# One remainder modulo 512 bytes for every operand that TensorE reads from SBUF

## The chip, the core and the metric

The kernel runs on one core of a Trainium2 chip. The time is that of the device, in microseconds, from one launch; several executions are timed, and their median is the figure. The kernel before takes 2820.65 us (three runs, 2819.92 to 2821.26).

## The reference

Two layers on 8 sequences of 3008 rows with 256 channels, in fp32 accuracy:

```python
X = np.fft.rfft(x, axis=1)                    # 3008 = 47 * 64
Yr = Xr @ w_r - Xi @ w_i + b_r
Yi = Xr @ w_i + Xi @ w_r + b_i
Y  = soft(Yr) + 1j * soft(Yi)                 # soft threshold at 0.01
y  = np.fft.irfft(Y, n=3008, axis=1)
t  = y.reshape(24064, 256)
out = (sigmoid(t @ w_gate) * (t @ w_val)) @ w_out     # d_ff = 1536
```

## The kernel before

The Fourier transform is a product with a 47-point table (`fa_sb`, line 176), then one with 64-point tables (`mf_sb`, line 237); between them the data goes through DRAM. The complex mixing (lines 271 and 293) follows, then the way back (`mi_sb`, lines 305 to 310, and `fb_sb`, line 340). The gated layer has its two first matrices split into a high and a low part (`w1h`, `w1l`), and the second likewise (`w2`); each product is three matmuls, high by high, high by low, low by high. Their operands are of type fp32r (one pass of TensorE); the four transforms at lines 176, 237, 305 and 340 are plain fp32, which TensorE runs as two passes, so the trace shows two matmul records for each.

The kernel runs in three stages, which the texts below name by number:

- **Stage 1**, the first 105 us: the first sequence's transform, in plain fp32, with the mixing by `mix4` (line 293).
- **Stage 2**, 105 to 1071 us: the transforms of the other seven sequences as side work (`fwd_b`, `mix`, `inv_b`, `inv_a`), put between steps of the gated layer for the first 4608 tokens (`ffn1`, lines 399 to 401, moving operands `yth` and `ytl`; `ffn2`, lines 427 to 429, moving operands `hh` and `hl`). A planner hands out the side work by fixed weights per step.
- **Stage 3**, 1071 us to the end: the gated layer for the other 19456 tokens, two blocks of 512 tokens at a time with Strassen's scheme of seven products. Its unit is a *half* (`half`, 228 of them). On TensorE a half is 33 matmuls of 512 columns: twelve in the first four products (`a11`, `s2`, `s3`, `s1`; line 659), twelve in `second` (lines 634 to 636, weights `w2`, moving `hh` and `hl`), nine in the last three products (`a12`, `s4`, `a22`; line 659 again). The four sums of a half gather in the PSUM banks `pa`, `pb`, `pc`, `pd`. Of `pd` there is one buffer only: the next half's `s3` product may start once VectorE's addition at line 720 has read it.

On VectorE, the last three additions or products of a half are lines 710, 714 and 720 in that order. On ScalarE, `put` (line 616) copies finished outputs at the end of each pair of blocks, once in twelve halves.

All memory in SBUF comes from pools. `const` and the pools `cw`, `p2`, `p4` grow from the lower end, `p0`, `p3`, `p5` (`side="right"`) from the upper end downwards. In every partition a tile is one run of bytes, and the address of a tile is the same in all partitions. The built program lists the addresses. Each matmul reads two operands from SBUF, the moving one and the stationary one (the weights). Modulo 512 bytes they start at:

| tiles | remainder before |
|---|---|
| `w1h`, `w1l`, `w2`, `th`, `tl`, `fa_sb`, `fb_sb` (weights or tables), `a11` to `a22`, `s1` to `s4`, `spare` (moving) | 128 |
| `hh`, `hl` in stages 2 and 3, `xf0`, `wi_sb` | 480 |
| `yth`, `ytl`, `vf`, `w_sb` | 0 |
| `xf`, `xfh`, `mf_sb`, `zf`, `xsh`, `xsl`, `yc`, `yh`, `yl`, `mi_sb`, `zero` | 32 |

A slice of a tile that TensorE reads begins a multiple of 512 bytes after the tile, but for the weights of `mix4` (line 293), half of which begin 256 bytes later.

Three `ffn2` steps of stage 2 are left over and run in the first halves of stage 3; their moving operand lies in `spare`, not in `hh` and `hl`:

```python
if c == NPL - 1 and f >= NF - BEHIND:
    hh, hl = (spare[f - NF + BEHIND][:, i, :CW] for i in range(2))
```

Of the kernel before, what the change touches and what calls it, by code (L numbers as in the profile page):

```python
# [9 lines left out]
F32 = mybir.dt.float32  # L10
# [9 lines left out]
R2, R1 = 47, 64  # L20
NK2 = 24
NQ = 2 * NK2
# [87 lines left out]
def tile_fft_mix_ffn(ctx: ExitStack, tc, x, w_r, w_i, b_r, b_i, w_one, w_out, mf, mi, mis, fa, fb, out):  # L110
# [3 lines left out]
    P = 128  # L114
    XR = x.shape[2]
    CT = D // P
# [4 lines left out]
    UT = 2 * PT  # L121
# [6 lines left out]

    const = ctx.enter_context(tc.tile_pool(name="const", bufs=1))

    p0s = ExitStack()
    p0 = p0s.enter_context(tc.tile_pool(name="p0", bufs=1, side="right"))
    p3s = ExitStack()
    fft = ExitStack()
    cw = fft.enter_context(tc.tile_pool(name="cw", bufs=1))
# [5 lines left out]
    def bank(name, tag="fft", bufs=FFT_BANKS):  # L141
        return (psf if tag == "fft" else psl).tile([P, 512], F32, tag=tag, bufs=bufs, name=name)
# [4 lines left out]
    def r2k(name):  # L147
        return p2.tile([P, 2, D], F32R, tag="r2k", bufs=NR2K, name=name)

    fa_sb = cw.tile([2 * R2, 2 * NQ], F32, name="fa_sb")  # L150
    nc.scalar.dma_start(fa_sb, fa)

    zd = [tc.dram_tile([NQ, R1, D], F32, name=f"zd{b}") for b in range(B)]
# [174 lines left out]
    def split_y(c, at, n, y):  # L328
        if c not in yts:
            yts[c] = [p3.tile([P, CT, CW], F32R, name=t) for t in ("yth", "ytl")]  # L330
        yh, yl = (t[:, :, at:at + n] for t in yts[c])
        nc.scalar.copy(yh, y)
        sub(yl, y, yh)

    def inv_a(u):
        vf = held.pop(("v", u))
        pa = bank("pia")[:, :CT * UT].rearrange("p (c h k) -> p c h k", c=CT, h=2)
        for hh in range(2):
            for ct in range(CT):
                nc.tensor.matmul(pa[:, ct, hh], vf[:, hh, ct * P:(ct + 1) * P], fb_sb[:, :PT], start=True, stop=True)  # L340
        py = pa.rearrange("p c h k -> p c (h k)")
        lo = u * UT
        n = 0
        if lo < T0:
            c, at = divmod(lo, CW)
            n = min(UT, CW - at)
        if 0 < n < UT and lo + n < T0:
            t = p3.tile([P, CT, UT], F32, name="carry", bufs=1)[:, :, :UT - n]
            nc.scalar.copy(t, py[:, :, n:])
            held["carry", c + 1] = t, UT - n  # L350
        if n:
            split_y(c, at, n, py[:, :, :n])
        if lo + UT > T0:
            t = result("yf")
            t = t[:, :CT * (UT - n)].rearrange("p (c k) -> p c k", c=CT)
            nc.scalar.copy(t, py[:, :, n:])
            nc.sync.dma_start(yd[:, :, lo + n - T0:lo + UT - T0], t)

    def result(name):
        return p3.tile([P, CW], F32, tag="ry", bufs=NYF, name=name)  # L360
# [123 lines left out]
    def ffn_units():  # L484
        units, todo = [], {}
        seq = [(c, f) for c in range(NPL) for f in range(NF)]

        def own(c):

            return range(-(-c * CW // UT), -(-(c + 1) * CW // UT))  # L490

        for c in range(1, NPL):
            at = (c - 1) * NF
            for i, u in enumerate(own(c)):
                todo.setdefault(at + (0, 3, 6)[i], []).append(lambda u=u: load_v(u))
                todo.setdefault(at + (3, 6, 9)[i], []).append(lambda u=u: inv_a(u))
            todo.setdefault(at + 1, []).append(lambda c=c: carry(c))

        def unit(n):
            c, f = seq[n]  # L500
            if n == 0:
                for i, u in enumerate(own(0)):
                    if i == 1:
                        w = w1h[:, 0].rearrange("p i t n -> p (i t n)")
                        keep_warm(bank("warm", "l1", L1_BANKS), w[:, :P], w, WARM_V)
                    inv_a(u)
            ffn1(c, f)
            for t in todo.pop(n, ()):
                t()
            if n >= LAG and n - LAG < len(seq) - BEHIND:  # L510
                ffn2(*seq[n - LAG])
        return [lambda n=n: unit(n) for n in range(len(seq))], own(0), own(NPL - 1)[-1] + 1
# [228 lines left out]

    bias_sb = cw.tile([P, 2, D], F32, name="bias_sb")
    bias4 = p0.tile([P, D], F32, name="bias4")
    ebias = cw.tile([P, 1], F32, name="ebias")
    fb_sb = const.tile([2 * NQ, P], F32, name="fb_sb")
    w1h = const.tile([P, NF, 2, CT, P], F32R, name="w1h")
    w1l = const.tile([P, NF, 2, CT, P], F32R, name="w1l")
# [183 lines left out]
    p3 = p3s.enter_context(tc.tile_pool(name="p3", bufs=2, side="right", reuse_waits="tile"))  # L931
# [18 lines left out]
    def inverse(g):  # L950

        us = [u for b in g for u in range(b * H // 2, (b + 1) * H // 2) if u >= u0]
        ahead = min(NVF - 1, len(us))

        def begin():
            for u in us[:ahead]:
                load_v(u)

        def go(i):
            if i + ahead < len(us):  # L960
                load_v(us[i + ahead])
            inv_a(us[i])
        return [(0.0, begin)], [(0.65, lambda i=i: go(i)) for i in range(len(us))]

    def behind(g):

        loads, units = inverse(g)
        return (loads, 0.05, 0.05), (units, 0.1, 1)

    def merge(*streams):  # L970

        return [u for _, _, u in sorted(((lo + (hi - lo) * (i + 0.5) / len(s), k, u) for k, (s, lo, hi) in
                                         enumerate(streams) for i, u in enumerate(s)), key=lambda t: t[:2])]

    (a3, q3), (a4, q4) = (fft_units(g, {}) for g in groups[3:])
    n = len(a3) // 3
    side = (merge((second_fft, 0, 1), (a3[:n], 0.2, 1)) +
            merge((third_fft, 0, 1), (a3[n:], 0, 0.85), *behind(groups[1])) +
            merge((q3, 0, 1), (a4, 0, 0.85), *behind(groups[2])) +
            merge((q4, 0, 1), *behind(groups[3])))  # L980
# [9 lines left out]
    for j in range(NF, len(ffn)):  # L990
        c, f = divmod(j, NF)
# [39 lines left out]
    a, b, c, d = banks[0]  # L1031
# [4 lines left out]
    with tc.manual_schedule():  # L1036
        for k in range(2 * NPR * NH):
            p, e = divmod(k, 2 * NH)
# [18 lines left out]
        n = NPR * NH  # L1057
# [36 lines left out]
```

## Time and profile before

| what | value |
|---|---|
| median of the runs | 2820.65 us |
| span of the profiled execution, and mean granted clock | 2819.0 us, 0.999 |
| TensorE busy | 2802.4 us (99%), 13896 matmul records |
| VectorE, ScalarE, GpSimd busy | 2082.3 (74%), 1309.6 (46%), 710.5 us (25%) |
| DMA, mean over the span | 85 GB/s |

The profile holds one execution. The only time it gives for it is the span from the first to the last instruction, 2819.0 us, which is 1.65 us under the median of the runs. A row of instructions has the line and engine, the operation, "out<-in" by tile name, the shapes, the count, then the summed busy time and the mean of one in ns, then the idle time ahead of it and what ended that. Matmuls overlap, so "mean ns of one" of a matmul (some 390 ns for 512 columns) is longer than the distance between two starts; the distance is read from the starts in the timeline. "PE" is the matmuls, "PEld" the loads of weights ahead of them.

### The profile page before, as it was taken

Reading aid. Unit: us, or ns where it says so; the run is one execution under the profiler, and the core shown is the slowest. Engines: PE = TensorE matmul, PEld = TensorE weight load, DVE = VectorE, ACT = ScalarE, POOL = GpSimd, SP = SyncE. Lnnn points to the kernel's source line nnn. Section 1 sums busy time; section 2 is a strip of 40 time slices with the busy share of each in tenths; the row PEclk is TensorE's granted clock in tenths of the full one; section 3 lists DMA queues with packets and bytes.
Section 4 is the critical chain, followed back from the end, with each engine's and each line's share of the span. In section 5 each row is a group of like instructions: output and inputs, shape, how many; then the busy total and the mean of one; then the engine's idle time right before and its main releaser. Section 6 shows DMA issues by size and latency. Waiting matters only on the chain.

```text
span 2819.0 us, 38251 instructions
## 1 busy us (share of the span) xinstructions
PE 2802.4 (99%) x13896; PEld 2308.1 (82%) x13896; DVE 2082.3 (74%) x3109; ACT 1309.6 (46%) x2276; POOL 710.5 (25%) x638
## 2 busy tenths in 40 slices
PE   9999999999999999999999999999999999999999
PEld 6678888888899888888888888888888888888887
DVE  5777778667787536777777777777777777777776
ACT  4664544545455444444444444444444444444443
POOL 0211010224100002333333333333333343333321
PEclk9999999999999999999999999999999999999999
DMA  9866544666554661000000000000000000000000
GB/s 296 257 213 194 170 143 149 199 184 192 165 152 140 186 187 38 30 15 16 30 31 27 4 31 31 31 16 15 31 30 16 15 30 31 30 1 30 30 16 15
DMA packets 173469, 241.01 MB, mean 85 GB/s; under 512 B 14592, under 2 KB 124896, under 8 KB 173280
## 3 DMA queue, kind: packets, MB, share of 16 engines
q1 hardware_dynamic: 163776, 214.93, 24.8%
q0 software_dynamic: 9408, 23.60, 2.5%
q8 instruction: 110, 1.80, 0.3%
q14 instruction: 79, 0.65, 0.1%
q10 hardware_dynamic: 96, 0.04, 0.0%
HBM read 134.17 MB, written 104.33 MB: 85 GB/s over the span
## 4 chain that ended last, share of the span: by engine, by line
PE 94%; DVE 2%; DMA 2%; ACT 1%; issue 0%; SPq 0%; DVEq 0%; ACTq 0%
PE pd L659 11%; PE pa L659 11%; PE pc L659 11%; PE po L636 8%; PE po L635 8%; PE po L634 8%; PE pm L271 6%; PE pb L659 5%; PE pia L340 4%; PE pb L237 3%; PE pa L176 2%; PE pg L399 2%; PE pg L401 2%; PE pg L400 2%; PE pv L399 2%; PE pv L400 2%
## 5 line engine op out<-in xcount | busy, mean ns | idle before, releaser
L636 PE MATMUL po<-hl,w 128*128 128x512 f32 x912 | 362.5, 397 | 0.0
L635 PE MATMUL po<-hh,w 128*128 128x512 f32 x912 | 361.5, 396 | 0.0
L634 PE MATMUL po<-hh,w 128*128 128x512 f32 x912 | 360.8, 396 | 0.0
L718 POOL TENSOR_TENSOR c<-c,c 128x512 f32<-128x512 f32 x114 | 147.7, 1296 | 831.0 <-DVE c L714 640.1
L659 PE MATMUL pa<-a,w1h 128*128 128x512 f32 x912 | 284.0, 393 | 0.0
L659 PE MATMUL pc<-s,w1h 128*128 128x512 f32 x912 | 283.7, 392 | 0.0
L714 DVE TENSOR_TENSOR c<-u,pc 128x512 f32<-128x512 f32 x228 | 156.7, 687 | 114.7 <-PE pc L659 106.2
L689 DVE TENSOR_TENSOR u<-u,pb 128x512 f32<-128x512 f32 x228 | 155.3, 681 | 88.8 <-PE pb L659 62.6
L606 ACT CAST hh<-v 128x512 fp32r<-128x512 f32 x114 | 70.7, 620 | 306.2 <-DVE v L699 306.2
L636 PEld LDWEIGHTS po<-hl,w 128*128 128x128 f32 x912 | 171.5, 188 | 41.9
L634 PEld LDWEIGHTS po<-hh,w 128*128 128x128 f32 x912 | 172.0, 189 | 40.9
L635 PEld LDWEIGHTS po<-hh,w 128*128 128x128 f32 x912 | 171.0, 188 | 40.8
L659 PEld LDWEIGHTS pa<-a,w1h 128*128 128x128 f32 x912 | 171.2, 188 | 40.1
L659 PEld LDWEIGHTS pc<-s,w1h 128*128 128x128 f32 x912 | 171.0, 188 | 37.6
L610 POOL TENSOR_TENSOR hl<-c,hh 128x512 fp32r<-128x512 f32 x114 | 152.4, 1337 | 186.1 <-ACT hh L606 186.1
L271 PE MATMUL pm<-w_sb,xsh 128*128 128x256 f32 x1008 | 189.4, 288 | 1.4 <-ACT xf L177 1.1
L659 PE MATMUL pc<-s,w1l 128*128 128x512 f32 x456 | 177.5, 389 | 0.0
L659 PE MATMUL pa<-a,w1l 128*128 128x512 f32 x456 | 177.0, 388 | 0.0
L720 DVE TENSOR_TENSOR u<-u,pd 128x512 f32<-128x512 f32 x228 | 156.9, 688 | 24.5 <-DVE c L714 0.9
L693 DVE TENSOR_TENSOR v<-v,pc 128x512 f32<-128x512 f32 x228 | 156.6, 687 | 24.4 <-DVE v L691 0.5
L691 DVE TENSOR_TENSOR v<-u,pd 128x512 f32<-128x512 f32 x228 | 156.9, 688 | 24.0 <-DVE u L689 0.5
L685 ACT COPY u<-pa 128x512 f32<-128x512 f32 x228 | 133.7, 586 | 78.7 <-PE pa L659 78.6
(174 smaller groups left out, 6738.7 us busy)
## 6 DMA issues: line engine op xcount, KB each, us to landing
zf<-zd SPq DMA_DIRECT2D x96, 256.0 KB, 3.6
vf<-vd SPq DMA_DIRECT2D x128, 192.0 KB, 3.1
out_dram<-ot SPq DMA_DIRECT2D x93, 256.0 KB, 2.2
vd<-vz SPq DMA_DIRECT2D x84, 256.0 KB, 2.9
ypair<-yd SPq DMA_DIRECT2D x19, 1024.0 KB, 5.0
yd<-yf SPq DMA_DIRECT2D x103, 188.0 KB, 3.0
xf<-in_x_dram SPq DMA_DIRECT2D x48, 384.0 KB, 4.1
zd<-xf SPq DMA_DIRECT2D x44, 384.0 KB, 3.4
```

What stands on the lines that cost most here:

```text
L271: nc.tensor.matmul(o, l, r, start=(i == 0), stop=(i == len(mms) - 1))
L610: sub_(hl, h, hh)
L634: nc.tensor.matmul(o, wh, hh, start=(f == 0), stop=False)
L635: nc.tensor.matmul(o, wl, hh, start=False, stop=False)
L636: nc.tensor.matmul(o, wh, hl, start=False, stop=(f == NF - 1))
L659: nc.tensor.matmul(o, l, r, start=not more and l is wh and r is xh, stop=l is wl, skip_group_check=more)
L689: add(u, u, b)
L691: add(v, u, d)
L693: add(v, v, c)
L714: add(c12, u, c)
L718: nc.gpsimd.tensor_mul(c12, g12, c12)
L720: add(u, u, d)
```

## The change

Four edits, all of them to where tiles lie:

```diff
+    edge = ctx.enter_context(tc.tile_pool(name="edge", bufs=1, side="right"))
+    edge.tile([P, 88], F32, name="edge")
     p0s = ExitStack()
     p0 = p0s.enter_context(tc.tile_pool(name="p0", bufs=1, side="right"))
...
-    fa_sb = cw.tile([2 * R2, 2 * NQ], F32, name="fa_sb")
+    fa_sb = cw.tile([2 * R2, P], F32, name="fa_sb")[:, :2 * NQ]
...
-            t = p3.tile([P, CT, UT], F32, name="carry", bufs=1)[:, :, :UT - n]
+            t = p3.tile([P, 3 * P], F32, name="carry", bufs=1)[:, :CT * UT].rearrange("p (c k) -> p c k", c=CT)[:, :, :UT - n]
...
-    ebias = cw.tile([P, 1], F32, name="ebias")
+    ebias = cw.tile([P, P], F32, name="ebias")[:, :1]
```

A tile `edge` that nobody uses takes 352 bytes at the upper end of each partition, so that everything in `p0`, `p3` and `p5` lies 352 bytes lower. The table `fa_sb` goes from 384 to 512 bytes, `ebias` from 4 to 512, `carry` from 1504 to 1536. In the built program every operand of TensorE then starts at remainder 128 modulo 512, but for the same half of the weights of `mix4`, which are at 384.

The instructions of each engine stand in the same order as before, with the same shapes and counts: 13214 on TensorE, 4426 on VectorE, 3199 on ScalarE, 1482 on SyncE. What each waits for is the same too, but for three waits of GpSimd on DMAs, before additions at line 586 in the first pair of stage 3, where a neighbouring tile's old transfer is now another one; one of these waits is an instruction more.

## The prediction

> **What bounds the kernel now.** First the table by stretch, cut at the stages (busy us of each engine with counts, then the granted clock, the DMA share and GB/s):
>
> ```profile
> 0.00:105.00 105.00, 97.30 (x546) 72.87 (x546) 68.07 (x116) 52.13 (x94) 12.86 (x23) 1.00 0.90 276
> 105.00:1071.00 966.00, 961.44 (x5805) 818.43 (x5804) 676.92 (x1167) 484.90 (x836) 125.52 (x189) 1.00 0.59 178
> 1071.00:2819.00 1748.00, 1743.64 (x7549) 1416.83 (x7548) 1337.35 (x1826) 772.54 (x1346) 572.08 (x426) 1.00 0.07 23
> ```
>
> TensorE has a gap of 4.4 us in all of stage 3, and VectorE, the next, works 1337 of 1748 us. The list of waits of TensorE in stage 3 has one entry, for the one buffer of `pd`:
>
> ```profile
> PE pd L659 <- DVE u L720: 0.4, 1, 0.4
> ```
>
> So stage 3 lasts as long as its matmuls stand apart: 1743.64 us by 7549 are 231.0 ns each. All have 512 columns and one pass, the clock is 1.00, and yet they aren't equal. The groups of TensorE in that window, different shapes apart:
>
> ```profile
> L636 PE MATMUL po<-hl,w 128*128 128x512 f32 x912 | 362.5, 397 | 0.0
> L635 PE MATMUL po<-hh,w 128*128 128x512 f32 x912 | 361.5, 396 | 0.0
> L634 PE MATMUL po<-hh,w 128*128 128x512 f32 x912 | 360.8, 396 | 0.0
> L659 PE MATMUL pa<-a,w1h 128*128 128x512 f32 x912 | 284.0, 393 | 0.0
> L659 PE MATMUL pb<-s,th 128*128 128x512 f32 x456 | 140.4, 389 | 0.0
> L428 PE MATMUL po<-spare,w 128*128 128x512 f32 x6 | 2.3, 389 | 0.0
> ```
>
> `pb`, with both operands at remainder 128, takes 389 ns; the `po` rows, with the moving operand at 480 and `w2` at 128, 396 to 397. Line 428 is the comparison within one line of code: from `spare` (128) 389 ns, while the same line in stage 2 reads `hh` at 480 and takes 396:
>
> ```profile
> L428 PE MATMUL po<-hh,w 128*128 128x512 f32 x210 | 83.1, 396 | 0.0
> ```
>
> The distances come from the starts in the timeline, here one half of stage 3 and a piece of the first halves:
>
> ```profile
> 2006.08 0.62 PE L659 MATMUL pa<-a,w1h 128*128 128x512 f32 x2
> ...
> 2008.80 0.40 PE L634 MATMUL po<-hh,w 128*128 128x512 f32 x1
> ...
> 2011.62 0.63 PE L659 MATMUL pa<-a,w1h 128*128 128x512 f32 x2
> ...
> 2013.69 0.62 PE L659 MATMUL pa<-a,w1h 128*128 128x512 f32 x2
> ```
>
> ```profile
> 1075.18 0.39 PE L427 MATMUL po<-spare,w 128*128 128x512 f32 x1
> ...
> 1076.54 0.62 PE L659 MATMUL pa<-a,w1h 128*128 128x512 f32 x2
> ```
>
> The first twelve matmuls of the half (all at 128) take 2008.80 − 2006.08 = 2.72 us, **226.7 ns** each. The twelve of `second` take 2.82 us, 235 each. The nine after them, again at 128, take 2.07 us, 230 each: the disturbance outlives its cause and dies out within nine matmuls. The six from `spare` take 1.36 us, 226.7 each. What two reads could meet is seen in the loads:
>
> ```profile
> 2045.31 0.41 PEld L659 LDWEIGHTS pd<-s,th 128*128 128x128 f32 x2
> ```
>
> ```profile
> 2045.31 0.39 PE L659 MATMUL pb<-s,tl 128*128 128x512 f32 x1
> 2045.53 0.62 PE L659 MATMUL pd<-s,th 128*128 128x512 f32 x2
> ```
>
> The weights for `pd` are loaded from the moment at which the matmul before begins to stream. I take it that the two reads disturb each other least when they start at the same remainder.
>
> [...]
>
> **The change part by part.** The base is the span of 2819.0 us; a run's median is 1.65 us more.
>
> *Stage 3.* A half now takes 2013.69 − 2006.08 = 7.61 us; 33 × 226.7 ns are 7.48. That is 0.13 us by 228 halves: **−29.6 us**. The whole stretch at 226.7 instead of 231.0 ns would give 7549 × 4.3 = 32.5; this also counts a few stalls that stay. Below, 0 if address has no part in it.
>
> *Stage 2, 512 columns.* `yth` goes from 0, `hh` from 480 to 128. An undisturbed run:
>
> ```profile
> 866.23 0.40 PE L399 MATMUL pg<-yth,w1h 128*128 128x512 f32 x1
> ...
> 869.72 1.05 PE L237 MATMUL pb<-mf_sb,zf 128*128 128x128 f32 x8
> ```
>
> 15 matmuls in 3.49 us, 232.7 each. Of such there are 1296 at lines 399 to 401 and 630 at 427 to 429, less those from `spare`, some 1910: 6.0 ns on each would be 11.5 us. But these runs have 6 to 18 matmuls and follow other shapes; if each has to settle like the nine above (230 ns), a run of 18 saves 18 × 6.0 − 9 × 3.3 = 78 of 108 ns, a run of six only 16 of 36. I take **−7 us**, between −3 and −11.5.
>
> *256 columns, the part against the change.* The products of line 271 (moving 0, weights 32) and those of lines 308 to 310, which have 32 and 32 already:
>
> ```profile
> 862.03 0.28 PE L271 MATMUL pm<-w_sb,xsl 128*128 128x256 f32 x1
> ...
> 863.92 0.28 PE L308 MATMUL pi<-yh,mi_sb 128*128 128x256 f32 x1
> ```
>
> ```profile
> 280.96 0.28 PE L309 MATMUL pi<-yl,mi_sb 128*128 128x256 f32 x1
> ...
> 281.56 0.59 PE L176 MATMUL pa<-xf,fa_sb 94*96 94x512 f32 x1
> ```
>
> Line 271: 16 in 1.89 us, 118.1 ns. The equal remainders: 5 in 0.60 us, 120.0. So here alignment costs some 1.9 ns, on 1512 matmuls of line 271, the 288 of line 293 (half of them) and, for settling sooner, a little on the 504 of lines 308 to 310: **+3 us**, between 0 and +3.5. A gain is not seen at any equal pair of this width.
>
> *The one buffer of `pd`.* TensorE gets faster, VectorE's chain of lines 710, 714, 720 does not. A usual half:
>
> ```profile
> 2042.57 0.39 PE L659 MATMUL pa<-a,w1l 128*128 128x512 f32 x1
> ```
>
> ```profile
> 2042.99 0.69 DVE L710 TENSOR_TENSOR g<-g,pa 128x512 f32<-128x512 f32 x1 [0.39 <-PE pa L659]
> 2043.75 0.69 DVE L714 TENSOR_TENSOR c<-u,pc 128x512 f32<-128x512 f32 x1
> 2044.55 0.69 DVE L720 TENSOR_TENSOR u<-u,pd 128x512 f32<-128x512 f32 x1
> ```
>
> The chain ends at 2045.24, and the load for `pd` starts at 2045.31, 0.07 later. From `pa` at 2042.57 to `pd` at 2045.53 TensorE has 13 matmuls in 2.96 us; at 226.7 they take 2.95. Only 0.01 to 0.02 of the 0.07 go, about what the signal needs to spare. If the load slipped in each of the some 95 odd halves and the matmuls had to settle again (0.03 us as above), it would cost 2.9: **+0.5**, between 0 and +2.9. Once in twelve halves ScalarE's output copies hold the chain up:
>
> ```profile
> 2006.75 0.58 ACT L616 COPY ot<-po 128x512 f32<-128x512 f32 x1 [0.66 <-DMA out_dram<-ot]
> ```
>
> ```profile
> 2012.72 0.68 DVE L710 TENSOR_TENSOR g<-g,pa 128x512 f32<-128x512 f32 x1
> 2014.10 0.69 DVE L720 TENSOR_TENSOR u<-u,pd 128x512 f32<-128x512 f32 x1
> ```
>
> Here line 720 ends at 2014.79, and there is no slack. From that copy the chain keeps its pace, while TensorE's matmuls up to then get some 0.13 us quicker. In these 19 halves up to 0.13 us is given back: **+1.5**, between 0 and +2.5. Next late then is `pd`'s `s3` product, with VectorE's line 720 as what ends the wait.
>
> *Nothing:* the unused 352 bytes and the padding move no data; `fa_sb` is loaded once, the same bytes; three waits of GpSimd name older transfers, and GpSimd has 572 us of work in 1748. Of the two-pass products line 237 has equal remainders (32 and 32) and 128 columns, line 340 unequal ones (128 and 0) and 94 columns, and they come out alike at 275 and 273 ns, so I count nothing there. Stage 1 waits for DMA at 0.90 share, whatever TensorE does.
>
> ```profile
> L340 PE MATMUL pia<-fb_sb,vf 96*128 96x94 f32 x1011 | 128.2, 273 | 1.2 <-DVE ys L277 0.5 <-DVE yt L273 0.5 <-ACT xsf L249 0.2
> L237 PE MATMUL pb<-mf_sb,zf 128*128 128x128 f32 x672 | 88.6, 275 | 0.0
> ```
>
> Sum: −29.6 − 7 + 3 + 0.5 + 1.5 = −31.6; 2819.0 + 1.65 − 31.6 = **2789** us. Its own bounds: all gains and no cost, −32.5 − 11.5 = −44, 2777; least of both, −29.6 − 3 + 3.5 + 2.9 + 2.5 = −23.7, 2797.
>
> **The rivals.** *(A) VectorE becomes the bound of stage 3.* If a wait at `pd` comes up in every second half, not in each twelfth, 114 × 0.13 = 15 us of the 29.6 go back: 2804. Against it: VectorE waits 0.39 us for `pa` at line 710, so its chain starts from TensorE, not from its own backlog.
>
> *(B) Not the remainder but the region.* All moving operands with 226.7 ns lie lower in SBUF than `hh`, `hl`, `yth`. If distance or the upper region is what costs, nothing is gained: 2820 to 2824. Against it: line 271's `w_sb` lies low, is unequal and doesn't settle at one distance, while lines 308 to 310 do. [...]
>
> *(C) Equal remainders collide.* In the 256-column rows the equal pair is the slower one. The longest single distance in a `second` is 240 ns:
>
> ```profile
> 2009.74 0.40 PE L635 MATMUL po<-hh,w 128*128 128x512 f32 x1
> 2009.98 0.40 PE L636 MATMUL po<-hl,w 128*128 128x512 f32 x1
> ```
>
> If all of `hh`, `hl`, `yth` and `ytl` came to stand there, it would be 5 ns × 2736 in stage 3, 7 × 1910 in stage 2, and the 3 of line 271: +30, 2851. It decides from the point at which the `po` rows stay above 396 ns. `spare` at 389 speaks against it.
>
> **How the numbers follow.** Forecast 0.75, (A) 0.11, (B) 0.10, (C) 0.04. The range 2778 to 2803 holds the forecast but for its last edge and most of (A). A difference under 0.2% (5.6 us) can't be told from none here. Faster: forecast and (A), with a little of (B): 0.87; same 0.10; slower 0.03.
>
> **What would show it.** Right: the `po` rows at 389 ns, as `spare` now; a half of 7.48 us; stage 3 near 1718 us; line 428 at 389 to 392 in stage 2; distances of 120 ns at line 271; the wait of `pd` on line 720 with some 20 entries. Wrong: `po` still at 396 (B) or above (C); `pd` waiting in over 100 halves (A); line 271 faster than 118 ns.

## The result and the profile after

| | before | after |
|---|---|---|
| median of the runs | 2820.56 us (2819.92 to 2821.26, 4 runs) | 2789.93 us (2788.98 to 2792.41, 4 runs) |
| ratio | | 0.9893, 95% interval 0.9879 to 0.9907 |
| span of the profiled execution | 2819.0 us | 2788.3 us |

The change takes 30.6 us off the median and 30.7 us off the profiled span. The forecast was 2789 us. After the change all line numbers up to 130 stay, those behind `edge` grow by two (line 634 is now 636).

The table by stretch of the kernel after, cut at the stages again (busy us of each engine with counts, granted clock, DMA share, GB/s):

```profile
0.00:105.00 105.00, 98.45 (x541) 74.30 (x541) 68.00 (x116) 52.27 (x94) 12.85 (x23) 0.98 0.89 274
105.00:1066.50 961.50, 957.07 (x5811) 820.89 (x5810) 676.19 (x1167) 485.44 (x836) 125.92 (x189) 1.00 0.60 179
1066.50:2788.30 1721.80, 1716.68 (x7549) 1414.59 (x7547) 1337.64 (x1826) 771.76 (x1346) 571.18 (x426) 1.00 0.07 23
```

Stage 3 goes from 1748.0 to 1721.8 us (−26.2), stage 2 from 966.0 to 961.5 (−4.5). Stage 1 stays but for some 0.6 us: its 546th matmul starts at 104.98 us before and at 105.54 after, in a stretch with a granted clock of 0.98 instead of 1.00. VectorE does the same work as before in stage 3 (1337.64 against 1337.35 us), and TensorE is still busy but for 5 us. What changed is how far its matmuls stand apart: the groups of TensorE in stage 3.

```profile
L636 PE MATMUL po<-hh,w 128*128 128x512 f32 x912 | 354.9, 389 | 0.0
L638 PE MATMUL po<-hl,w 128*128 128x512 f32 x912 | 354.8, 389 | 0.0
L637 PE MATMUL po<-hh,w 128*128 128x512 f32 x912 | 354.8, 389 | 0.0
...
L661 PE MATMUL pa<-a,w1h 128*128 128x512 f32 x912 | 280.7, 389 | 0.0
...
L661 PE MATMUL pd<-s,th 128*128 128x512 f32 x456 | 143.0, 395 | 0.9 <-DVE u L722 0.9
```

The `po` rows, 396 to 397 ns before, now have 389 ns, and `pa` has come from 393 to 389: with the disturbance in `second` gone, the nine matmuls after it no longer have to settle: 2.04 us instead of 2.07. A half, seen in the starts of the timeline:

```profile
2002.71 0.61 PE L661 MATMUL pa<-a,w1h 128*128 128x512 f32 x2
...
2005.43 0.39 PE L636 MATMUL po<-hh,w 128*128 128x512 f32 x1
...
2008.15 0.61 PE L661 MATMUL pa<-a,w1h 128*128 128x512 f32 x2
...
2010.19 0.61 PE L661 MATMUL pa<-a,w1h 128*128 128x512 f32 x2
```

Twelve matmuls in 2.72 us, the twelve of `second` in 2.72 (2.82 before), nine more in 2.04 (2.07 before): 226.7 ns throughout, and 7.48 us for the half, as for most of the 228.

One group of stage 3 has become slower, `pd<-s,th`, from 391 to 395 ns (the row of after is the last one above, this is the one of before):

```profile
L659 PE MATMUL pd<-s,th 128*128 128x512 f32 x456 | 141.5, 391 | 0.4 <-DVE u L720 0.4
```

It is the product that needs the one buffer of `pd`. Its wait is on the load of the weights. The list of waits of the weight loads in stage 3, first before, then after:

```profile
PEld pd L659 <- DVE u L720: 3.2, 9, 0.8
```

```profile
PEld pd L661 <- DVE u L722: 8.3, 21, 0.8
```

In stage 2 the group of line 430 (before: 428) has come to 389 ns, while the 256-column group of line 273 (before: 271) is the slower by 2 ns, first before, then the two groups after:

```profile
L271 PE MATMUL pm<-w_sb,xsl 128*128 128x256 f32 x504 | 141.4, 281 | 0.0
```

```profile
L430 PE MATMUL po<-hh,w 128*128 128x512 f32 x210 | 81.7, 389 | 0.0
L273 PE MATMUL pm<-w_sb,xsl 128*128 128x256 f32 x504 | 142.4, 283 | 0.0
```

### The profile page after: what moved, and what is told of

Read it like the earlier page. It is cut to its first block, busy times and chain, and to the rows that moved or that the text cites. A ratio compares the mean times of both kernels' runs of the same rounds, so it can differ in the third digit from the quotient of the medians.

```text
span 2788.3 us, 38252 instructions
## 1 busy us (share of the span) xinstructions
PE 2772.2 (99%) x13896; PEld 2309.8 (83%) x13896; DVE 2081.8 (75%) x3109; ACT 1309.5 (47%) x2276; POOL 710.0 (25%) x638
## 4 chain that ended last, share of the span: by engine, by line
PE 96%; DVE 3%; DMA 1%; ACT 0%; issue 0%; SPq 0%; DVEq 0%; ACTq 0%
PE pd L661 11%; PE pc L661 11%; PE pa L661 11%; PE po L638 7%; PE po L636 7%; PE po L637 7%; PE pm L273 6%; PE pb L661 5%; PE pia L342 4%; PE pa L178 3%; PE pb L239 3%; PE pg L401 2%; PE pg L403 2%; PE pg L402 2%; PE pv L401 2%; PE pv L403 2%
## 5 line engine op out<-in xcount | busy, mean ns | idle before, releaser
L636 PE MATMUL po<-hh,w 128*128 128x512 f32 x912 | 354.9, 389 | 0.0
L638 PE MATMUL po<-hl,w 128*128 128x512 f32 x912 | 354.8, 389 | 0.0
L637 PE MATMUL po<-hh,w 128*128 128x512 f32 x912 | 354.8, 389 | 0.0
```

What stands on the lines that cost most here:

```text
L636: nc.tensor.matmul(o, wh, hh, start=(f == 0), stop=False)
L637: nc.tensor.matmul(o, wl, hh, start=False, stop=False)
L638: nc.tensor.matmul(o, wh, hl, start=False, stop=(f == NF - 1))
```

## The experiments

The theory: a matmul is slowed while it streams its moving operand and the next weights are loaded, by an amount that depends on the difference of the two addresses' remainders. Its rivals: the region of SBUF, the particular address 128, another modulus, and a share of the small lower tiles in the gain.

**The two halves of the change apart.** First the upper end alone (`edge` and `carry`; the table and the bias tile stay as they were):

```diff
-    fa_sb = cw.tile([2 * R2, P], F32, name="fa_sb")[:, :2 * NQ]
+    fa_sb = cw.tile([2 * R2, 2 * NQ], F32, name="fa_sb")
...
-    ebias = cw.tile([P, P], F32, name="ebias")[:, :1]
+    ebias = cw.tile([P, 1], F32, name="ebias")
```

> Only the 352 bytes at the upper end and the padded carry; the table and the bias tile stay small, so line 271 keeps 0 against 32 and lines 308 to 310 keep 32 against 32. Remainder theory: the po rows at 389 ns as in the changed kernel, stage 3 at 1716 us; line 271 back at 118.2 ns a matmul (119.7 in the changed kernel), which gives 2 to 3 us back: about 2787 us, faster than the full change. Rival (the settled state is carried from the 256-column products into the 512-column ones): lines 399 to 429 of stage 2 lose 2 to 4 us of their 7.6 us gain, about 2790 us. Rival (the small tiles carry the gain): about 2820 us.

Measured: 2786.84 us (ratio to the kernel before 0.9882, 0.9869 to 0.9896), 3.1 us under the full change; the intervals of the two overlap, so the difference rests on the profile. There line 273 is back where it was, and the `po` rows have the whole gain:

```profile
L636 PE MATMUL po<-hh,w 128*128 128x512 f32 x912 | 354.9, 389 | 0.0
...
L273 PE MATMUL pm<-w_sb,xsh 128*128 128x256 f32 x1008 | 189.3, 288 | 1.6 <-ACT xf L179 1.2 <-DVE ys L279 0.4
```

By the starts, undisturbed matmuls of line 273 stand 118.0 ns apart here and 119.7 in the full change. The rival of a settled state carried into the 512-column runs has a little to it: line 401's stand at 231.8 ns instead of 230.5, line 403's at 229.8 instead of 229.2, line 431's at 230.4 instead of 228.7, together some 1 us; line 402's go the other way by 0.3 ns, 0.1 us.

Then the lower tiles alone, put into the kernel before:

> Only the table and the bias tile widened; hh and hl stay at 480, yth and ytl at 0. Remainder theory: po rows at 396 ns as before, line 271 at 119.7 ns: 2 to 3 us slower than before, about 2823 us, which is inside what can be told from no change. Rival (the lower tiles carry part of the gain): 2810 us or less.

Measured: 2822.14 us (ratio 1.0006, 0.9998 to 1.0015): no change that can be told, and no gain. The `po` rows stay where they were, and line 271's group has come from 288 to 289 ns, 119.5 ns from start to start:

```profile
L636 PE MATMUL po<-hl,w 128*128 128x512 f32 x912 | 362.5, 397 | 0.0
...
L271 PE MATMUL pm<-w_sb,xsh 128*128 128x256 f32 x1008 | 191.2, 289 | 1.7 <-ACT xf L177 1.1 <-DVE ys L277 0.3 <-ACT yf L356 0.3
```

So all of the gain comes from the 352 bytes at the upper end. By the distances the other half of the change costs some 2 us (2.3 at line 273 and 0.5 at lines 310 to 312, less the 1 us that it spares in the 512-column runs), which the medians alone could not tell from nothing.

**Which remainder, and modulo what.** The changed kernel with other sizes of `edge`, so that `hh`, `hl`, `yth` and `ytl` lie at another distance from their weights, which stay at 128:

```diff
-    edge.tile([P, 88], F32, name="edge")
+    edge.tile([P, 24], F32, name="edge")     # 24, 56, 80 in three kernels
```

> The changed kernel with 96 instead of 352 bytes at the upper end: hh, hl, yth and ytl at remainder 384, 256 from their weights. If the remainder modulo 512 decides: po rows at 395 to 397 ns, a half of 7.61 us, about 2822 us. If 256 or a smaller power of two is enough: po rows at 389, a half of 7.48 us, about 2790 us. If the amount of the distance matters: a value of its own between.

> The same with 224 bytes: remainder 256, 128 from the weights. Modulo 512 or 256: po rows at 395 to 397 ns, about 2822 us; modulo 128 or less: 389 ns, about 2790 us.

> The same with 320 bytes: remainder 160, 32 from the weights. Any modulus of 64 or more: po rows over 389 ns. If the two reads only have to be close to each other: near 389, and less than at 128 and 256.

And one with everything moved by 32 bytes, so that the common remainder is 160:

```diff
+    const.tile([P, 8], F32, name="shift")
...
-    edge.tile([P, 88], F32, name="edge")
+    edge.tile([P, 80], F32, name="edge")
```

> An unused tile of 32 bytes at the lower end and 320 bytes at the upper: all operands at 160. If the difference of the two operands decides: as the changed kernel, po rows at 389, a half of 7.48 us, about 2790 us. If 128 itself is what is good (a multiple of 64 or 128): over 389 ns, up to 2822 us.

One run of each new size, beside one of 2819.47 us for the kernel before; the times of the first and the last row are the medians of four runs from above. In the kernel with 160 the lines of `second` are 637 to 639.

| moving operand minus weights | mean distance of lines 636 to 638 | a usual half | time |
|---|---|---|---|
| 0, both at 128 (the change) | 226.8 ns | 7.48 us | 2789.93 us |
| 0, both at 160 | 226.8 ns | 7.48 us | 2787.96 us |
| 256 | 226.8 ns | 7.48 us | 2789.75 us |
| 128 | 232.6 ns | 7.57 us | 2812.71 us |
| 32 | 233.5 ns | 7.60 us | 2817.80 us |
| 352 (before) | 234.5 ns | 7.61 us | 2820.56 us |

The groups of `po<-hh,w` over the whole program, first with both at 160, then at distances 256, 128 and 32:

```profile
L637 PE MATMUL po<-hh,w 128*128 128x512 f32 x912 | 355.0, 389 | 0.0
```

```profile
L636 PE MATMUL po<-hh,w 128*128 128x512 f32 x912 | 355.0, 389 | 0.0
```

```profile
L636 PE MATMUL po<-hh,w 128*128 128x512 f32 x912 | 359.6, 394 | 0.0
```

```profile
L636 PE MATMUL po<-hh,w 128*128 128x512 f32 x912 | 361.5, 396 | 0.0
```

The common remainder need not be 128: 160 does as well. And **the modulus is 256 bytes, not 512**, as far as these distances tell: 256 is as good as none (389 ns both), 128 isn't (394 ns). Being near does not help, 32 is worse than 128 (233.5 against 232.6 ns). The region of SBUF is not what counts either, since the kernels with distances 0, 128 and 256 differ by 128 and 256 bytes in the place of `hh` and `hl`, and only the middle one is slow (232.6 against 226.8 ns). The modulus that the change is written for is a sufficient one, not the smallest.

**Whose weights.** In the trace of before each load of weights in `second` starts with the matmul ahead, 2 to 4 ns after it. Whether a matmul suffers from its own weights or from the load of the next could not be told there, since all weights had one remainder. So in the changed kernel the low part of `w2` gets a tile of its own, 96 bytes off modulo 256, and in `second` only the middle matmul of each three (line 637) reads it, as line 430 does in stage 2. The lines that read and fill the two tiles are left out here:

```diff
...
-    w2 = const.tile([P, NF, 2, D], F32R, name="w2")
+    w2h = const.tile([P, NF, D], F32R, name="w2h")
+    const.tile([P, 40], F32, name="gap")
+    w2l = const.tile([P, NF, D], F32R, name="w2l")
+    const.tile([P, 24], F32, name="gap2")
...
```

> The changed kernel with the low part of w2 in a tile of its own, at remainder 32 modulo 256, 96 away from all else, so that in second only the weights of the middle matmul (line 637) are off. If a moving read is disturbed by the load of the next weights, it is the matmul ahead of them that stretches: coming from the settled rhythm, the first matmul of second (line 636) stands about 236 ns before the second one. If it is disturbed by its own weights, the first stays at 227 and the second (line 637) stretches. In both, disturbed matmuls come once in three and the rest is settling: po rows between 389 and 397 ns, a half of 7.52 to 7.60 us.

Measured: 2806.33 us in one run. The timeline of TensorE where a `second` begins out of the settled rhythm:

```profile
2014.44 0.40 PE L636 MATMUL po<-hh,w2h 128*128 128x512 f32 x1
2014.68 0.40 PE L637 MATMUL po<-hh,w2l 128*128 128x512 f32 x1
2014.91 0.39 PE L638 MATMUL po<-hl,w2h 128*128 128x512 f32 x1
2015.14 0.40 PE L636 MATMUL po<-hh,w2h 128*128 128x512 f32 x1
```

In whole nanoseconds the three distances here are 237, 233 and 230; the means over the 912 of each line are 236.3, 232.5 and 231.2. The first matmul, whose own weights are aligned, stretches at once, by 10 ns: it streams while `w2l` is loaded. So it is the load of the *next* weights that matters. The matmul that uses `w2l` and the one after it read as on the way back (233, 230); whether the first of them also suffers from its own weights can't be told apart from that. By the means, one disturbed load costs some 10 + 6 + 5 ns. The opposite reading, that the load is slowed and holds up the next matmul, finds no support: as recorded, the loads of `second` take 188 ns in the kernels before and after and in this one, and end 36 to 45 ns (medians) ahead of their matmuls.

**What was given back.** At 226.67 ns each, the 33 matmuls of 228 halves and the 18 from `spare` would take 1709.5 us. From the first matmul of line 661 to the last matmul of the program stage 3 takes 1715.9, which is 6.4 more. Long halves follow the output copies, which come once in twelve: of these 19, 16 last 7.69 us or more. One of them in the kernel after, first ScalarE, then VectorE and TensorE:

```profile
1805.63 1.55 ACT L618 COPY ot<-po 128x512 f32<-128x512 f32 x3
...
1808.34 0.59 ACT L618 COPY ot<-po 128x512 f32<-128x512 f32 x1 [0.65 <-DMA out_dram<-ot]
1808.82 0.63 ACT L718 ACTIVATE c<-c 128x512 f32<-128x512 f32 x1
1809.35 0.58 ACT L687 COPY u<-pa 128x512 f32<-128x512 f32 x1
```

```profile
1810.02 0.69 DVE L691 TENSOR_TENSOR u<-u,pb 128x512 f32<-128x512 f32 x1 [1.49 <-ACT u L687]
```

```profile
1815.69 0.69 DVE L722 TENSOR_TENSOR u<-u,pd 128x512 f32<-128x512 f32 x1
```

```profile
1815.00 0.62 PE L661 MATMUL pa<-a,w1h 128*128 128x512 f32 x2
...
1816.14 0.39 PE L661 MATMUL pb<-s,tl 128*128 128x512 f32 x1
1816.44 0.73 PE L661 MATMUL pd<-s,th 128*128 128x512 f32 x2
1817.01 0.39 PE L661 MATMUL pd<-s,tl 128*128 128x512 f32 x1
```

ScalarE's fourth output copy waits 0.65 us for a DMA, the copy of `pa` behind it is late, VectorE's line 691 waits for that copy, and line 722 ends at 1816.38. That is 0.24 us after 1816.14, the start of `pb`'s last matmul, with which the load for `pd` would start if it need not wait. From `pa` to `pd`'s third matmul are eight distances in 2.01 us, 0.20 more than 8 × 226.7 ns. To test the chain, the fourth copy is put behind the next half's copy of `pa` and its sigmoid, in the changed kernel:

```diff
-    after_m1, before_sums, before_second, after_gate = [], [], [], []
+    after_m1, before_sums, before_second, after_gate, after_u = [], [], [], [], []
...
                     if s and ct:
-                        after_gate.append(todo)
+                        (after_gate if p == NPR - 1 else after_u).append(todo)
...
         run(before_sums)
         run(after_m1)
+        run(after_u)
```

> The changed kernel, with the fourth output copy of each pair of blocks run on ScalarE after the copy of pa and the sigmoid of the next half instead of before them. Theory (that copy, waiting for a DMA, holds up VectorE's chain, and the load for pd is late by some 0.2 us once in twelve halves): those halves fall from 7.69 to 7.48 us, 19 times 0.21 is 4 us: about 2786 us. [...] Rival (the late copy holds its PSUM bank too long): a new wait at line 636, over 2790 us.

Measured: 2783.82 us (ratio to the kernel before 0.9872, 0.9859 to 0.9886), 6.1 us under the changed kernel. Every half after an output copy now lasts 7.48 us, and the waits for `pd` fall from 21 to 5 (lines behind the edit stand one further down here, 723 for 722):

```profile
PEld pd L661 <- DVE u L723: 2.1, 5, 0.8
```

```profile
1804.60 0.64 ACT L719 ACTIVATE c<-c 128x512 f32<-128x512 f32 x1
1805.18 0.59 ACT L687 COPY u<-pa 128x512 f32<-128x512 f32 x1
1805.66 0.63 ACT L725 ACTIVATE u<-u 128x512 f32<-128x512 f32 x1
1806.19 0.58 ACT L618 COPY ot<-po 128x512 f32<-128x512 f32 x1
```

The copy is no longer ahead of `pa`'s, and waits for nothing. Stage 3 takes 1711.3 us, 4.6 less than in the changed kernel; no new wait at line 636 came up. The other 1.5 us lie outside stage 3, where nothing was changed; they stay open, and are less than these medians can tell. The same edit in the kernel before:

> The kernel before, with the late fourth output copy alone. Theory (the wait for pd came to matter only with the faster matmuls): the halves after an output copy fall from 7.64 to 7.61 us, 19 times 0.03 to 0.05 is at most 1 us: no change that can be told, about 2819.5 us. Rival (the copy cost as much before): 4 us less, about 2816 us.

Measured: 2818.60 us (ratio 0.9997, 0.9988 to 1.0006): no change that can be told. The halves after the copies fall from 7.64 to 7.61 us, as expected. From its first matmul of line 659 to the last matmul, stage 3 takes 1741.3 us where the kernel before takes 1742.2: there the late copy is worth 0.9 us, against 4.6 in the changed kernel. It is the faster matmuls that made the copy count.

**Both together**, the upper end alone and the late copy:

> Both of the two: upper end alone, and the late copy. If they add up: about 2783 us, 7 us under the changed kernel. If line 271's 2 to 3 us are not real, 2786; if the copy's 4 us are not, 2787.

Measured: 2782.65 us (2781.82 to 2783.74; ratio to the kernel before 0.9866, 0.9851 to 0.9881), the fastest of all, 7.3 us under the change. In the profile the two add up, line 273 at 118.0 ns and stage 3 at 1711.3 us; the median is 1.2 us under that of the late copy alone, less than line 273's 2.3 us and less than these runs can tell apart.

## Why the prediction was right

*The bound and the base.* Right. TensorE sets the end in all of stage 3, and the distance of its matmuls is what the change moved.

*Stage 3, −29.6 us.* The step, 33 × 226.7 ns by half, came out: 7.48 us in most halves. In three digits a usual half went from 7.613 to 7.480, which over 228 halves is 30.4 us; the 29.6 were rounded down. What `spare` and the first twelve matmuls of a half showed in the trace of before held for the whole program.

*Stage 2, −7 us.* The tight matmuls of lines 401 to 403 and 429 to 431 (before: 399 to 401 and 427 to 429) stand 1.9 to 6.8 ns nearer each other. Counted over all 1926 matmuls of these lines, that is 7.6 us. That the short runs would not settle wholly was right too: the means go from 226.7 ns (line 430) to 230.5 (line 401).

*256 columns, +3 us.* Line 273 went from 118.2 to 119.7 ns, 1430 undisturbed matmuls, +2.1 us; lines 310 to 312 from 119.0 to 120.0, +0.5. The sign was that of the five distances at line 309, and the size nearly: 1.5 ns at line 273 instead of 1.9.

*The one buffer of `pd`, +0.5 us.* Right that the usual odd halves would just hold: the load starts 65 to 69 ns after line 722's end, where it was 75 to 81 after line 720's, and a load that waits starts 51 to 54 ns after.

*The halves after an output copy, +1.5 us with at most 2.5.* This is the step that was mis-sized. In the kernel after they cost 4.6 us, as the late copy shows by taking them away; 0.9 of that they cost before, so what the change gave back is some 3.7. The mechanism and the place were right, with 21 late loads where some 20 were named. But the shift was counted from the fourth copy on, 0.13 us. The chain hangs on the first three copies, in the half ahead; from there to the load for `pd` there are 10.79 us before (2004.04 to 2014.83) and 10.51 after (1805.63 to 1816.14), which is 0.28 us. The chain itself, to the end of line 720 or 722, takes 10.75 us in both (to 2014.79 and to 1816.38). So these halves didn't only lose their gain, they got longer than before, 7.69 against 7.64 us.

The other terms made up for it, and that is luck: the gain of the usual halves and that of stage 2 were taken 0.8 and 0.6 us too small, the loss at 256 columns 0.4 too large. In all, −26.3 in stage 3, −7.6 and +2.6 in stage 2, and some +0.6 that is lost in stage 1 give the −30.7.

*The rivals.* (A) was wrong as a whole, but right in one half in twelve. (B), the region, fell: `hh` and `hl` lie as high as before, but for 352 bytes, and have 389 ns. Of (C) only this is true: at 256 columns the equal pair is the slower one, 119.7 ns at line 273 against 118.2 at line 271 before. These 512-column fp32r matmuls stand 226.8 against 232.6 to 234.5 ns apart by nothing but the place of the moving operand, and the stretch falls first on the matmul during which the next weights are loaded: 236.3 ns at line 636 where only the weights of line 637 are off. By what mechanism the load and the moving read disturb each other, no run here tells.

## What to carry to other kernels

Where equal matmuls have unequal distances in one trace, compare the addresses of the moving operand and of the weights loaded meanwhile: at equal remainders modulo 256 bytes, 512-column fp32r matmuls here went from 234.5 to 226.8 ns, and the price was one unused tile. At 256 columns equal remainders cost 1.5 ns against the one unequal pair that was run (0 and 32), so align by stage and not on principle. A trace often holds the experiment already, as the six matmuls from `spare` did. And when the bounding engine gets faster, measure each fixed chain of the other engines from the point where it really hangs, which is not always the last wait that the trace shows in it.

## What the runs showed of the hardware

- At 512 columns the modulus is 256 bytes, by the distances that were run. Distances of 0 and 256 give 226.8 ns, 128 gives 232.6, 32 gives 233.5, 352 (96 modulo 256) 234.5.
- The disturbance has a memory. In the kernel with `w2l` apart one load that is off stretches the matmul over it by 10 ns and the two after it by 6 and 5 (means), and the row of twelve in `second` of the kernel before leaves the next eight aligned matmuls at 224 to 236 ns before they are back at 227. A wait has such an echo, too: after the late load for `pd` at 1816.44 us, with all operands aligned, the distances are 337, 231, 231, 235, 229, 232 and 231 ns, then 227.
- At 256 columns the aligned rhythm is the slower one: 120.0 ns (lines 310 to 312 after the change) against 118.0 (line 273 with the upper end alone). The aligned distance at 512 columns is 226.7 ns, 106.7 more than at 256. An estimate from these two distances alone, which takes the growth as even, leaves 120.0 − 106.7 = 13.3 ns of either that do not grow with the columns. What they are made of no run here tells.
